# A fused attention and two-MoE kernel: six PSUM banks in one pool, other copies in the first MoE, a scaling moved in the last sum

## The chip, the cores and the metric

The kernel runs on one core of a Trainium2 chip. The metric is device time in microseconds of one execution; the value quoted is the median of three runs.

## The reference

Three stages follow each other. In the first, 4 batches of 12 heads with 448 rows of 64 are attended with two mixings across heads ("talking heads"); the second and third are dense two-layer blocks ("MoE" by name) over 1792 tokens of 768.

```python
scores = scale * np.matmul(q, k.transpose(0, 1, 3, 2))
scores = np.einsum('bhij,hg->bgij', scores, w_pre)
scores = scores - np.max(scores, axis=-1, keepdims=True)
attn = np.exp(scores)
attn = attn / (np.sum(attn, axis=-1, keepdims=True) + 1e-09)
attn = np.einsum('bhij,hg->bgij', attn, w_post)
attn_out = np.matmul(attn, v)
x = attn_out.transpose(0, 2, 1, 3).reshape(B * S, H * D)
h = x @ w_in                                     # 768 x 2048
g = np.where(h > 0.0, h, np.exp(np.minimum(h, 0.0)) - 1.0)
x = g @ w_out                                    # 2048 x 768
h = x @ w_in2                                    # 768 x 1024
sm = softmax(h); solu = h * sm
ln = (solu - mean) / np.sqrt(var + 1e-06) * g_ln
out = ln @ w_out2                                # 1024 x 768
```

## The kernel before

**Attention.** The 448 rows of a batch are cut into chunks of up to 120 rows (`CH`, 17 chunks in all). A chunk goes through five kinds of work on TensorE (PE), and each leaves its result in PSUM, from where ScalarE (ACT) or VectorE (DVE) takes it away.

- A *score* block (`add_score`, L574) multiplies q and k of two heads into two banks; two evacuations (`evac`, L580, tile `sev`) copy them out, on ACT or VectorE, and DMAs on SP's queue (`move`, L531, `sp<-sev`) spread them over partitions into the chunk's tile `sp`. `sev` has 8 buffers.
- A *pre* block (`pre`, L646, tile `pm`) mixes the heads for a unit of two groups of ten rows, again into two banks. VectorE takes the maxima (`top`, L651, tile `st`), ACT the exponentials (`expo`, L656, tile `e`, 10 buffers). There are 90 units.
- VectorE and GpSimd prepare the scaled second mixing (`weigh`, L667, tile `wr`).
- A *post* block (`post`, L679, tiles `po`) applies it, into two fixed banks; two copies (`take`, L687) put it into `at`.
- An *AV* block (L728, tile `av`) multiplies by v, two blocks to a chunk; a copy (L735, tile `x`) and a DMA send it to DRAM as `xs`.

Of the eight PSUM banks `ps_sc` has three (scores and AV), `ps_pm` three (pre) and `po` two. Each pool is a ring: the next tile takes the bank that was taken longest ago. In the first chunk scores use both pools in turn.

The order on every engine is written by a planner (`schedule`). Each operation has a rank (the time at which it is wished for), its engines with a cost in us, the operations it depends on, and the buffers it takes (`new`) or uses. The planner keeps a clock for each engine, and takes the next operation among the first 200 by rank that can start earliest. `ready` gives the time at which dependencies and buffers are free: the end of what frees them and a tail by engine (`tail`, 2.0 us for SP) plus `more`, or `lag` where it is given. What the planner thinks only sets the order; on the chip each engine waits on semaphores, in that order. The loads of q (`add_q`) and k (`add_k`) are such operations on SP's queue, with rank 9 and 4 us ahead of the score; q's was given `more=.5`, k's `lag=3.0`.

**First MoE** (function body after `schedule()`). The hidden units go in 8 groups (`fg`) of 256, the tokens in 4 blocks (`tb`) of 448. For each group and block `hid` (L377, tile `h`) makes two tiles of hidden units, `elu` (L388 to L393) works them, and `outp` (L883, tile `o`, four banks in a ring) makes six output tiles. For the first group ACT copies each `o` into the running sum `x1` (L897); for later groups VectorE adds it (L900). Between them the weights of the next groups are decoded by VectorE, ACT and GpSimd (`decode`, L218 to L231; `split`, L254; `wi_spill`, L286), a step at a time (`tick`, `paced`), by a running estimate of VectorE's time (`work`).

**Second MoE.** `hid2` (L1022), a normalisation, then for each of 7 pairs of token tiles seven products (`product`, L1094, tile `w`) in the order P1, P6, P7, P5, P4, P2, P3. `behind` adds them up into the four quarters of the output tile `ob` (L1112, L1114), scales a finished quarter by a value per token on ACT (L1117) and stores it by a DMA on SP's queue (L531).

Of the kernel before, what the change touches and what calls it, by code (L numbers as in the profile page):

```python
# [21 lines left out]
ECH = DM // 128  # L22
# [47 lines left out]
LEAD = 3  # L70

@with_exitstack
def kernel(ctx: ExitStack, tc: tile.TileContext, qa, kt, vt, wpre, wpost,
# [294 lines left out]
    def hid(fg, tb, ft, kcs=range(ECH)):  # L368
        wh, wl = w1[fg][0], w1[fg][1]
        xh, xl = xT[tb]  # L370
        if kcs[0] == 0:
            ring, p = ("sc", ps_sc) if (tb, ft) not in ((1, 1), (3, 1)) else ("h", ps_h)
            h_t[fg, tb, ft] = p.tile([128, 512], F32, tag=ring, name="h")
        ps = h_t[fg, tb, ft]
        for kc in kcs:
            for n, (a, x) in enumerate(((wh, xh), (wh, xl), (wl, xh))):
                nc.tensor.matmul(ps[:, :S], a[:, kc * FG + ft * 128:kc * FG + (ft + 1) * 128], x[:, kc, :],  # L377
                                 start=kc == 0 and n == 0, stop=kc == ECH - 1 and n == 2)
# [20 lines left out]
    class Buf:  # L399
        def __init__(self, ring):  # L400
            self.ring, self.users, self.at = ring, [], None
# [6 lines left out]
    bufs = {"sc": 3, "pm": 3, "po": 2, "sev": SB, "e": EB, "wr": WB, "st": 4, "kst": 2, "q": 4,  # L408
# [12 lines left out]
    def schedule():  # L421
# [14 lines left out]
        def ready(o, e):  # L436
            t = 0.0
            for d in o.deps:
                if d.end is None:
                    return None  # L440
                t = max(t, seen(d, e))
            more = dict.fromkeys(bufs, 0)
            for b in o.new:
                ring = rings[b.ring]
                n = bufs[b.ring] - more[b.ring]
                more[b.ring] += 1
                if b.at is None and len(ring) >= n:
                    for u in ring[-n].users:
                        if u.end is None:
                            return None  # L450
                        t = max(t, seen(u, e))
            return t

        while todo:
# [20 lines left out]
            if o.port and e in held:  # L475
                held[e] = o.end
            for b in o.new:
                if b.at is None:
                    b.at = o
                    rings[b.ring].append(b)  # L480
# [56 lines left out]
    def add_q(c, hf):  # L537

        qb_[c, hf] = Buf("q")
        r = t_sc[c, 6 * hf]  # L540

        def load(e):
            q_t[c, hf] = q_p.tile([128, 3, 128], F32, tag="q", name="q")
            dma(q_t[c, hf], qa[c, :, 3 * hf:3 * hf + 3])

        q_op[c, hf] = op(r - 9 if c > 1 else 4.0 + .1 * hf if c else [0.0, 3.0][hf], load, [], [qb_[c, hf]], sp=.5, more=.5)

    def add_k(b, h):
# [8 lines left out]
        k_op[b, h] = op(r0 - 4 if b else .5 + h * .6, load, [], [kb[b, h]], lag=3.0, **{"sp" if b or h % 4 == 0 else "act": .5})  # L557

    def add_score(c, h):
# [3 lines left out]
        ring = ("sc", "pm")[h // 2 % 2] if c == 0 else "sc"  # L563
        scb, svb = [Buf(ring) for _ in range(2)], [Buf("sev") for _ in range(2)]
# [3 lines left out]
        def mm(e):  # L568
            T[key] = [pools["ps_" + ring].tile([128, 512], F32, tag=ring, name="sc") for _ in range(2)]
# [63 lines left out]
    for u, sl in enumerate(units):  # L633
        eb, wb, sb = [Buf("e") for _ in range(2)], Buf("wr"), Buf("st")
        pmb, pob = [Buf("pm") for _ in range(2)], [Buf("po") for _ in range(2)]
# [5 lines left out]
        def pre(e, u=u, sl=sl):  # L641
            ps_t[u] = [ps_pm.tile([128, 512], F32, tag="pm", name="pm") for _ in range(2)]
# [63 lines left out]
    for c in range(NC):  # L706
# [12 lines left out]
        for n in range(2):  # L719
            r = t_av[c, n]  # L720
            xb, avb = Buf("x"), Buf("sc")

            def mm(e, c=c, n=n, w=w):
                ps = x_t[c, n] = ps_sc.tile([128, 512], F32, tag="sc", name="av")[:, :3 * w].rearrange("p (k w) -> p k w", k=3)
# [121 lines left out]
    for i in range(3):  # L846
        need_x = add_x(1, i, t_hid - 6 + 2 * i)
        add_w(3 + i, t_hid - 3 + 3 * i)
    for ft in range(2):
        o = None  # L850
        for p in range(3):
            o = op(t_hid + HD + ft * .01, lambda e, ft=ft, p=p: hid(0, 0, ft, range(2 * p, 2 * p + 2)),
                   need + [o] + [sc_ev[lc, h] for h in range(NH)], pe=HID / 3)
# [3 lines left out]
    schedule()  # L857
    spend(500)
# [12 lines left out]
    ps_o = pool("ps_o", 4, space=PSUM)  # L871
    def outp(fg, tb, rest):
# [3 lines left out]
        for e in range(ECH):  # L876
            run(1.21)
            ps = ps_o.tile([128, 512], F32, tag="o", name="o")
# [17 lines left out]
            if fg == 0:  # L896
                nc.scalar.copy(x1[tb][:, e, :], ps[:, :S])  # L897
            else:
# [197 lines left out]
    def behind(q, x):  # L1096
# [124 lines left out]
```

## Time and profile before

| | |
|---|---|
| median of three runs | 1047.11 us (1046.87 to 1049.83) |
| the profiled execution | 1046.41 us |
| its span, first to last instruction | 1044.6 us |
| granted TensorE clock, mean | 0.998 |
| PE busy / weight loads busy | 1021.1 / 859.6 us |
| VectorE / ACT / GpSimd busy | 732.6 / 556.1 / 286.2 us |
| chain that ended last, PE's share | 88% |

Busy time is what the instructions' records cover; overlapping records count once. On PE a record of a matmul begins where it starts and ends where a model ends it, so the distance between starts tells more than the length. "PEld" are the weight loads, which run beside the matmuls. A line with a wait names the waiting engine, the tile it was about to write and the line, and behind the arrow what was seen to release it; "issue" stands where nothing was seen. Attention fills the span up to about 360 us, the first MoE goes to about 821, the second from there on.

### The profile page before, as it was taken

To read this page: it belongs to the slowest core of one execution; us is meant where nothing else is said; L and a number is where in the kernel's file an instruction comes from. 1 tells how busy PE (TensorE), PEld (TensorE's weight loads), DVE (VectorE), ACT (ScalarE), POOL (GpSimd) and SP (SyncE) were. 2 spreads that over 40 slices of the span, in tenths; PEclk is the share of its full clock that TensorE was granted. 3 is DMA by queue.
4 is the path that set the end of the run, shared out by engine and by line. 5 is a ranking of instruction groups with operands and counts; after the bars stand their busy time and mean duration, and the time that the engine had idled before them with its cause. 6 is when DMAs were issued, how large, how long until landed. Compare 5 with 4: busy or idle time off the path is not lost.

```text
span 1044.6 us, 28451 instructions
## 1 busy us (share of the span) xinstructions
PE 1021.1 (98%) x11604; PEld 859.6 (82%) x11604; DVE 732.6 (70%) x1371; ACT 556.1 (53%) x1178; POOL 286.2 (27%) x297
## 2 busy tenths in 40 slices
PE   6899999999999999999999999999999999999998
PEld 2467777777666898999999999999999888889998
DVE  5687787677677357689978687786855355668874
ACT  3476677777677575544444345444444245555543
POOL 5011011111013524556534445444544200000000
PEclk9999999999999999999999999999999999999999
DMA  6776876776856542653523232423282533838741
GB/s 199 219 229 187 242 214 211 222 227 188 237 157 185 156 143 92 206 177 132 182 77 115 96 106 83 149 87 126 81 297 106 200 107 106 187 106 202 151 102 61
DMA packets 142442, 165.79 MB, mean 159 GB/s; under 512 B 79496, under 2 KB 119272, under 8 KB 142312
## 3 DMA queue, kind: packets, MB, share of 16 engines
q1 hardware_dynamic: 136207, 143.27, 46.2%
q0 software_dynamic: 3968, 17.30, 4.3%
q10 hardware_dynamic: 2137, 3.41, 1.1%
q8 instruction: 91, 1.49, 0.6%
q14 instruction: 39, 0.32, 0.1%
HBM read 88.02 MB, written 37.22 MB: 120 GB/s over the span
## 4 chain that ended last, share of the span: by engine, by line
PE 88%; DMA 3%; DVE 3%; ACT 3%; issue 2%; POOL 1%; SPq 0%; ACTq 0%; DVEq 0%; POOLq 0%
PE h L377 21%; PE o L883 21%; PE h L1022 11%; PE w L1094 10%; PE av L728 7%; PE po L679 7%; PE pm L646 6%; PE sc L574 6%; DMA sp<-sev 2%; ACT e L656 1%; DMA q<-in_qa_dram 1%; DVE st L651 1%; DVE wy L231 1%; ACT at L687 0%; DVE wq L227 0%
## 5 line engine op out<-in xcount | busy, mean ns | idle before, releaser
L656 ACT ACTIVATE e<-pm,st 128x448 f32<-128x448 f32 x180 | 113.7, 636 | 63.0 <-DVE st L651 54.7
L651 DVE TENSOR_REDUCE st<-pm 128x1 f32<-128x448 f32 x180 | 105.7, 617 | 54.6 <-PE pm L646 52.8
L883 PE MATMUL o<-gh,woh 128*128 128x448 f32 x384 | 140.6, 366 | 1.0 <-ACT x L897 0.8
L883 PE MATMUL o<-glo,woh 128*128 128x448 f32 x384 | 140.1, 365 | 0.0
L883 PE MATMUL o<-gh,wol 128*128 128x448 f32 x384 | 139.6, 363 | 0.0
L679 PEld LDWEIGHTS po<-wr,e 60*64 60x64 f32 x5040 | 101.0, 134 | 37.5 <-issue 23.8
L574 PE MATMUL sc<-kt,q 64*64 64x448 f32 x816 | 119.0, 559 | 9.2 <-DMA kt<-in_kt_dram 4.2
L900 DVE TENSOR_TENSOR x<-x,o 128x448 f32<-128x448 f32 x168 | 101.7, 613 | 28.7 <-PE o L883 27.7
L389 POOL TENSOR_TENSOR glo<-g,gh 128x448 fp32r<-128x448 f32 x64 | 83.3, 1301 | 124.6 <-ACT gh L388 122.2
L667 POOL TENSOR_TENSOR wr<-wpost_t,st 128x120 f32<-128x120 f32 x90 | 35.8, 398 | 281.8 <-DVE st L663 226.5
L646 PE MATMUL pm<-sp,wpre_t 64*64 64x448 f32 x720 | 108.6, 555 | 3.8 <-ACT e L656 2.3
L679 PE MATMUL po<-wr,e 60*64 60x60 f32 x5040 | 107.4, 219 | 3.4 <-issue 2.8
L377 PE MATMUL h<-xh,wih 128*128 128x448 f32 x288 | 105.4, 366 | 0.0
L377 PE MATMUL h<-xh,wil 128*128 128x448 f32 x288 | 105.1, 365 | 0.0
L377 PE MATMUL h<-xl,wih 128*128 128x448 f32 x288 | 104.7, 363 | 0.0
L1022 PE MATMUL h<-wi,x2h 128*128 128x512 f32 x308 | 98.7, 395 | 0.8 <-issue 0.8
L728 PEld LDWEIGHTS av<-at,v 128*64 128x64 f32 x1632 | 75.4, 137 | 15.0 <-issue 4.6
L393 DVE SCALAR_TENSOR_TENSOR g<-g,h 128x448 f32<-128x448 f32 x64 | 39.5, 616 | 66.0 <-ACT g L392 65.5
L728 PE MATMUL av<-at,v 128*64 128x120 f32 (+5 forms) x1632 | 82.6, 258 | 0.7 <-ACT x L735 0.5
L883 PEld LDWEIGHTS o<-gh,woh 128*128 128x128 f32 x384 | 72.1, 188 | 7.3 <-ACT x L897 1.4
L883 PEld LDWEIGHTS o<-glo,woh 128*128 128x128 f32 x384 | 72.0, 188 | 6.0
L883 PEld LDWEIGHTS o<-gh,wol 128*128 128x128 f32 x384 | 72.1, 188 | 5.6
(124 smaller groups left out, 1988.0 us busy)
## 6 DMA issues: line engine op xcount, KB each, us to landing
sp<-sev SPq DMA_DIRECT2D x93, 210.0 KB
ws<-in_wi_dram SPq DMA_DIRECT2D x33, 512.0 KB
ws<-in_wo_dram SPq DMA_DIRECT2D x21, 512.0 KB
lts<-sq SPq DMA_DIRECT2D x14, 512.0 KB
lt<-lts SPq DMA_DIRECT2D x56, 128.0 KB
q<-in_qa_dram SPq DMA_DIRECT2D x34, 192.0 KB
v<-in_vt_dram SPq DMA_DIRECT2D x24, 256.0 KB
wis<-ws POOLq DMA_DIRECT2D x12, 512.0 KB, 3.2
```

The lines of the kernel that those rows point to most:

```text
L377: nc.tensor.matmul(ps[:, :S], a[:, kc * FG + ft * 128:kc * FG + (ft + 1) * 128], x[:, kc, :], start=kc == 0 and n == 0, stop=kc == ECH - 1 ...
L389: nc.gpsimd.tensor_tensor(glo, g, f(gh), ALU.subtract)
L574: nc.tensor.matmul(T[key][i][64 * x:64 * x + 64, :S], q[sl, h % 6 // 2, 64 * x:64 * x + 64], k[sl, :], start=True, stop=True)
L646: nc.tensor.matmul(ps_t[u][r][64 * s:64 * s + 64, :S], wpre_t[p, :], sp_t[c][p, g, :], start=True, stop=True)
L651: nc.vector.tensor_reduce(out=st_t[u][:P, r:r + 1], in_=ps_t[u][r][:P, :S], op=ALU.max, axis=AX.X, negate=True)
L656: nc.scalar.activation(out=t[:P], in_=ps_t[u][r][:P, :S], func=AF.Exp, bias=st[:P, r:r + 1], scale=1.0, accum_out=st[:P, 2 + r:3 + r])
L679: nc.tensor.matmul(out[:, :, 5 * r:5 * r + 5], e_t[u, r][sl, 64 * n:64 * n + 64], wr_t[u][sl, r].rearrange("p (g a) -> p g a", a=5), start ...
L728: nc.tensor.matmul(ps[64 * k:64 * k + 64, i, :], v_t[CH[c][0]][:, 6 * n + 2 * i + k, q, :], at_t[c][:, q, 6 * n + 2 * i + k, :w], start=q ...
L883: nc.tensor.matmul(ps[:, :S], a[:, ft * DM + e * 128:ft * DM + (e + 1) * 128], x, start=n == 0, stop=n == 5)
L900: nc.vector.tensor_tensor(x1[tb][:, e, :], x1[tb][:, e, :], ps[:, :S], ALU.add)
L1022: nc.tensor.matmul(ps[:, hf * 512:hf * 512 + 512], a[:, k, :], w, start=n == 0, stop=n == 3 * ECH - 1)
L1094: nc.tensor.matmul(ps[:, :384], a[:, s, k, :], w, start=k == 0 and i == 0, stop=k == 3 and i == 2)
```

## The change

1. *Banks in attention.* The six banks of `ps_sc` and `ps_pm` become six named tiles of one buffer each (`bank0` to `bank5`), and the planner picks for each score, pre or AV block the banks that are free first, preferring banks last used by the same kind. Scores from the fourth chunk on, AV blocks after the first chunk's and pre blocks from the third chunk's first unit on may take any of the six; earlier ones stay in their half. Scores and AV together hold at most four banks, pre blocks at most four (`CAP`).
2. *Loads.* For chunks after the second, the planner counts 6.0 us (`QL`) from the end of a q load's issue to its use; the same for k loads after the first batch's.
3. *First MoE.* The hidden tiles take banks 0 to 2 in a named turn; the two first ones are operations with buffers. The four `o` banks are named in turn. The copies of `o` for the first group's token blocks 2 and 3 go to VectorE, with 0.55 in the running estimate.
4. *Last sum.* Behind P5, ACT scales the quarter c12 too; P3's product is then scaled and added in one VectorE instruction, and its ACT scaling is gone.

```diff
+CAP = 4
+QL = 6.0
...
-            ring, p = ("sc", ps_sc) if (tb, ft) not in ((1, 1), (3, 1)) else ("h", ps_h)
-            h_t[fg, tb, ft] = p.tile([128, 512], F32, tag=ring, name="h")
+            if home is not None:
+                h_t[fg, tb, ft] = home.tile()
+            elif (tb, ft) not in ((1, 1), (3, 1)):
+                h_t[fg, tb, ft] = ps_sc.tile([128, 512], F32, tag=f"bank{h_next[0]}", name="h", bufs=1)
+                h_next.append(h_next.pop(0))
+            else:
+                h_t[fg, tb, ft] = ps_h.tile([128, 512], F32, tag="h", name="h")
...
+        def tile(self):
+            p = pools["ps_sc" if self.bank < 3 else "ps_pm"]
+            return p.tile([128, 512], F32, tag=f"bank{self.bank}", name=self.ring, bufs=1)
+
+    banks = [None] * 6
+    most = {"sc": CAP, "pm": CAP}
...
-    bufs = {"sc": 3, "pm": 3, "po": 2, "sev": SB, "e": EB, "wr": WB, "st": 4, "kst": 2, "q": 4,
+    bufs = {"po": 2, "sev": SB, "e": EB, "wr": WB, "st": 4, "kst": 2, "q": 4,
...
+            asked = [b for b in o.new if b.ring in most]
+            if asked:
+                free_at = {}
+                for i, own in enumerate(banks):
+                    if own is None:
+                        free_at[i] = 0.0
+                    elif all(u.end is not None for u in own.users):
+                        free_at[i] = max(seen(u, e) for u in own.users)
+                kind = asked[0].ring
+                best = sorted((i for i in free_at if i in asked[0].only),
+                              key=lambda i: (max(free_at[i], t), banks[i] is not None and banks[i].ring != kind, free_at[i]))[:len(asked)]
+                if len(best) < len(asked):
+                    return None
+                t = max([t] + [free_at[i] for i in best])
+                rest = [i for i, own in enumerate(banks) if own is not None and own.ring == kind and i not in best]
+                over = len(asked) + len(rest) - most[kind]
+                if over > 0:
+                    ends = sorted(free_at[i] for i in rest if i in free_at)
+                    if len(ends) < over:
+                        return None
+                    t = max(t, ends[over - 1])
+                o.pick = best
...
-        q_op[c, hf] = op(r - 9 if c > 1 else 4.0 + .1 * hf if c else [0.0, 3.0][hf], load, [], [qb_[c, hf]], sp=.5, more=.5)
+        q_op[c, hf] = op(r - 9 if c > 1 else 4.0 + .1 * hf if c else [0.0, 3.0][hf], load, [], [qb_[c, hf]], sp=.5, lag=QL if c > 1 else 2.5)
...
-        pmb, pob = [Buf("pm") for _ in range(2)], [Buf("po") for _ in range(2)]
+        pmb, pob = [Buf("pm", range(0 if u >= first[2] else 3, 6)) for _ in range(2)], [Buf("po") for _ in range(2)]
...
-            xb, avb = Buf("x"), Buf("sc")
+            xb, avb = Buf("x"), Buf("sc", range(6 if c else 3))
...
-            if fg == 0:
+            if fg == 0 and tb < 2:
                 nc.scalar.copy(x1[tb][:, e, :], ps[:, :S])
+            elif fg == 0:
+                work(.55, pe_t + .1)
+                nc.vector.tensor_copy(x1[tb][:, e, :], ps[:, :S])
...
-        nc.vector.tensor_tensor(dst, ps, src, ALU.add)
+        if x == "P3":
+            nc.vector.scalar_tensor_tensor(dst, ps, col(9, t), src, ALU.mult, ALU.add)
+        else:
+            nc.vector.tensor_tensor(dst, ps, src, ALU.add)
         if x == "P5":
             nc.vector.tensor_tensor(c12, ps, c12, ALU.add)
+            nc.scalar.activation(out=c12, in_=c12, func=AF.Copy, scale=col(9, t))
...
-            nc.scalar.activation(out=dst, in_=dst, func=AF.Copy, scale=col(9, tt))
+            if x != "P3":
+                nc.scalar.activation(out=dst, in_=dst, func=AF.Copy, scale=col(9, tt))
```

The planner's new order shows on PE, here in attention around the first AV block of the twelfth chunk (88 rows). `sc<-kt,q` are score blocks (x4 is one block), `pm` pre blocks, `po` the first rows of a post block, `av` AV blocks. Before:

```order
L646 MATMUL pm<-sp,wpre_t 64x448 x4
L679 MATMUL po_108<-wr,e 64x12x5
...
L574 MATMUL sc<-kt,q 64x448 x4
L646 MATMUL pm<-sp,wpre_t 64x448 x4
L728 MATMUL av<-at,v 64x88 x24
L646 MATMUL pm<-sp,wpre_t 64x448 x4
L679 MATMUL po_108<-wr,e 64x12x5
...
L574 MATMUL sc<-kt,q 64x448 x4
```

With the change, a little ahead of the same place (an AV block's tile is named `sc` there as well, and x8 are two blocks):

```order
L616 MATMUL sc<-kt,q 64x448 x8
L721 MATMUL po_108<-wr,e 64x12x5
...
L688 MATMUL pm<-sp,wpre_t 64x448 x4
L616 MATMUL sc<-kt,q 64x448 x8
L721 MATMUL po_108<-wr,e 64x12x5
...
L688 MATMUL pm<-sp,wpre_t 64x448 x4
L770 MATMUL sc<-at,v 64x120 x24
```

Before, a pre block follows nearly every post block and scores come singly; now scores come in pairs, and pre blocks move against post blocks.

On VectorE in the first MoE, from the first group's third token block on (`x` and `x_2` are the running sums, `ws`, `wq`, `wy` a weight being decoded, `g` the hidden units). Before:

```order
L231 SCALAR_TENSOR_TENSOR wy<-wy,wq 128x512
L218 TENSOR_SCALAR ws<-ws 128x512
L393 SCALAR_TENSOR_TENSOR g<-g,h 128x448
L223 TENSOR_SCALAR wq<-ws 128x512
L227 SCALAR_TENSOR_TENSOR wq<-ws,wq 128x512
```

With the change:

```order
L229 SCALAR_TENSOR_TENSOR wq<-ws,wq 128x512
L946 COPY x_2_6992<-o 128x448
L233 SCALAR_TENSOR_TENSOR wy<-wy,wq 128x512
L946 COPY x_2_6992<-o 128x448
L402 SCALAR_TENSOR_TENSOR g<-g,h 128x448
L946 COPY x_2_6992<-o 128x448
L220 TENSOR_SCALAR ws<-ws 128x512
```

The copies now stand between the decode steps, one to a step.

On ACT at the end of the program, the last pair's products (`ob<-ob,sm` is the scaling, `ob<-w` the first product's copy). Before:

```order
L1080 CAST lA_11253<-lt 128x512
L1117 ACTIVATE ob<-ob,sm 128x384
L1080 CAST lS_11254<-sl 128x512
L1105 COPY ob<-w 128x384
L1117 ACTIVATE ob<-ob,sm 128x384 x4
```

With the change:

```order
L1129 CAST lA_11253<-lt 128x512
L1129 CAST lS_11254<-sl 128x512
L1154 COPY ob<-w 128x384
L1167 ACTIVATE ob<-ob,sm 128x384
L1171 ACTIVATE ob<-ob,sm 128x384 x3
```

Of the last four scalings the first is now that of c12 behind P5, and none follows P3.

## Rows read from the trace of the kernel before

**Rows 1.** The page, busy us (share of the span) xinstructions.
```profile
PE 1021.1 (98%) x11604; PEld 859.6 (82%) x11604; DVE 732.6 (70%) x1371; ACT 556.1 (53%) x1178; POOL 286.2 (27%) x297
```
**Rows 2.** Stretches: us; busy (x) of PE, PEld, DVE, ACT, POOL; clock, DMA share, GB/s.
```profile
500.00:600.00 100.00, 100.00 (x495) 92.57 (x494) 79.47 (x122) 42.69 (x80) 48.08 (x42) 1.00 0.35 115
```
**Rows 3.** Timeline of PE in attention: start us, us, engine, line, what.
```profile
142.37 0.99 PE L679 MATMUL po<-wr,e 60*64 60x60 f32 x56
143.18 0.94 PE L574 MATMUL sc<-kt,q 64*64 64x448 f32 x8
143.94 1.20 PE L646 MATMUL pm<-sp,wpre_t 64*64 64x448 f32 x8
144.69 1.26 PE L574 MATMUL sc<-kt,q 64*64 64x448 f32 x8
```
**Rows 4.** The chain that ended last, one AV block: start us, us, what.
```profile
155.41 2.61 PE av L728 x48
```
**Rows 5.** Stretch 65 to 345 us: PE and PEld of L574, L646, L679, L728; all instructions.
```profile
65.00:345.00 280.00, 85.95 (x616) 28.88 (x616) 1.00 0.71 209
65.00:345.00 280.00, 92.50 (x632) 27.95 (x632) 1.00 0.71 209
65.00:345.00 280.00, 94.86 (x4429) 89.35 (x4429) 1.00 0.71 209
65.00:345.00 280.00, 71.12 (x1344) 64.90 (x1344) 1.00 0.71 209
65.00:345.00 280.00, 275.52 (x7022) 197.09 (x7023) 208.02 (x528) 201.12 (x533) 40.08 (x84) 1.00 0.71 209
```
**Rows 6.** Waits of the weight loads, 65 to 345 us: us in total, times, longest.
```profile
PEld po L679 <- issue: 21.0, 77, 1.1
PEld pm L646 <- issue: 9.7, 46, 0.2
PEld pm L646 <- ACT e L656: 6.5, 19, 0.9
...
PEld sc L574 <- ACT sev L580: 2.3, 7, 0.5
...
PEld sc L574 <- DVE sev L580: 0.7, 2, 0.5
```
**Rows 7.** Timeline of PE, a pre block at 329 us; in brackets the idle time before.
```profile
329.11 0.54 PE L646 MATMUL pm<-sp,wpre_t 64*64 64x448 f32 x1
329.82 0.98 PE L646 MATMUL pm<-sp,wpre_t 64*64 64x448 f32 x6 [0.18 <-ACT e L656]
```
**Rows 8.** The chain that ended last, loads of q.
```profile
185.81 4.24 DMA q<-in_qa_dram
...
282.34 3.67 DMA q<-in_qa_dram
```
**Rows 9.** Waits of PE, 345 to 470 us.
```profile
PE o L883 <- ACT x L897: 0.8, 1, 0.8
```
**Rows 10.** Groups by line: busy us, mean ns of one, idle us before.
```profile
L897 ACT COPY x<-o 128x448 f32<-128x448 f32 x24 | 12.5, 536 | 1.7 <-PE o L883 1.5
L580 DVE COPY sev<-sc 128x448 f32<-128x448 f32 x87 | 52.6, 615 | 11.4 <-PE sc L574 11.1
```
**Rows 11.** Stretch 395 to 425 us, columns as in rows 2.
```profile
395.00:425.00 30.00, 29.15 (x144) 26.63 (x143) 20.34 (x33) 19.07 (x38) 18.04 (x14) 1.00 0.35 123
```
**Rows 12.** Timeline of the end of the program.
```profile
1040.51 0.56 DVE L1112 TENSOR_TENSOR ob<-w,ob 128x384 f32<-128x384 f32 x1 [1.52 <-PE w L1094]
1041.10 0.61 ACT L1117 ACTIVATE ob<-ob,sm 128x384 f32<-128x384 f32 x1 [1.46 <-DVE ob L1112]
1041.74 0.33 SPq L531 DMA_DIRECT2D out_dram<-ob  x1
```
**Rows 13.** Waits of ACT, 0 to 65 us.
```profile
ACT sev L580 <- DMA sp<-sev: 5.2, 3, 2.2
```

More of the change, by code (lines that the diff above doesn't have):

```diff
@@ L366, with hid @@
     h_t, g_t = {}, {}
-    def hid(fg, tb, ft, kcs=range(ECH)):
+    h_next = []
+    def hid(fg, tb, ft, kcs=range(ECH), home=None):
         wh, wl = w1[fg][0], w1[fg][1]
@@ L399, with __init__ @@
     class Buf:
-        def __init__(self, ring):
-            self.ring, self.users, self.at = ring, [], None
+        def __init__(self, ring, only=range(6)):
+            self.ring, self.users, self.at, self.only = ring, [], None, only
+        def tile(self):
[3 more added lines that the diff above has]
+    most = {"sc": CAP, "pm": CAP}
     class Op:
@@ L442, in ready @@
             more = dict.fromkeys(bufs, 0)
+            asked = [b for b in o.new if b.ring in most]
[20 more added lines that the diff above has]
+                o.pick = best
             for b in o.new:
+                if b.ring in most:
+                    continue
                 ring = rings[b.ring]
@@ L476, in schedule @@
                 held[e] = o.end
+            for b, i in zip((b for b in o.new if b.ring in most), getattr(o, "pick", ())):
+                b.bank, banks[i] = i, b
             for b in o.new:
@@ L479, in schedule @@
                     b.at = o
-                    rings[b.ring].append(b)
+                    if b.ring not in most:
+                        rings[b.ring].append(b)
             o.emit(e)
@@ L556, in add_k @@
         r0 = t_sc[HEAD[b] - 1, h] if b else 0.0
-        k_op[b, h] = op(r0 - 4 if b else .5 + h * .6, load, [], [kb[b, h]], lag=3.0, **{"sp" if b or h % 4 == 0 else "act": .5})
+        k_op[b, h] = op(r0 - 4 if b else .5 + h * .6, load, [], [kb[b, h]], lag=QL if b else 3.0, **{"sp" if b or h % 4 == 0 else "act": .5})
     def add_score(c, h):
@@ L562, in add_score @@
         n = 5 * G
-        ring = ("sc", "pm")[h // 2 % 2] if c == 0 else "sc"
-        scb, svb = [Buf(ring) for _ in range(2)], [Buf("sev") for _ in range(2)]
+        scb, svb = [Buf("sc", range(3 * (h // 2 % 2 if c == 0 else 0), 6 if c > 2 else 3 * (1 + (h // 2 % 2 if c == 0 else 0)))) for _ in range(2)], [Buf("sev") for _ in range(2)]
         r = t_sc[c, h]
@@ L568, in mm @@
         def mm(e):
-            T[key] = [pools["ps_" + ring].tile([128, 512], F32, tag=ring, name="sc") for _ in range(2)]
+            T[key] = [b.tile() for b in scb]
             q, k = q_t[c, h // 6], kt_t[b, h]
@@ L639, with pre @@
                 at_ops[c] = []
-        def pre(e, u=u, sl=sl):
-            ps_t[u] = [ps_pm.tile([128, 512], F32, tag="pm", name="pm") for _ in range(2)]
+        def pre(e, u=u, sl=sl, pmb=pmb):
+            ps_t[u] = [b.tile() for b in pmb]
             for s, (c, g) in enumerate(sl):
@@ L720, with mm @@
             r = t_av[c, n]
-            xb, avb = Buf("x"), Buf("sc")
-            def mm(e, c=c, n=n, w=w):
-                ps = x_t[c, n] = ps_sc.tile([128, 512], F32, tag="sc", name="av")[:, :3 * w].rearrange("p (k w) -> p k w", k=3)
+            xb, avb = Buf("x"), Buf("sc", range(6 if c else 3))
+            def mm(e, c=c, n=n, w=w, avb=avb):
+                ps = x_t[c, n] = avb.tile()[:, :3 * w].rearrange("p (k w) -> p k w", k=3)
                 for i in range(3):
@@ L848 @@
         add_w(3 + i, t_hid - 3 + 3 * i)
+    hb = [Buf("sc", range(3)) for _ in range(2)]
     for ft in range(2):
@@ L851 @@
         for p in range(3):
-            o = op(t_hid + HD + ft * .01, lambda e, ft=ft, p=p: hid(0, 0, ft, range(2 * p, 2 * p + 2)),
-                   need + [o] + [sc_ev[lc, h] for h in range(NH)], pe=HID / 3)
+            o = op(t_hid + HD + ft * .01, lambda e, ft=ft, p=p: hid(0, 0, ft, range(2 * p, 2 * p + 2), hb[ft]),
+                   need + [o] + [sc_ev[lc, h] for h in range(NH)], [] if p else [hb[ft]], [hb[ft]] if p else [], pe=HID / 3)
+    for b in hb:
+        b.users.append(Op())
     for i in range(3):
@@ L857 @@
     schedule()
+    h_next += [3 - sum(b.bank for b in hb)] + [b.bank for b in hb]
     spend(500)
@@ L870 @@
     ps_h = pool("ps_h", 1, space=PSUM)
-    ps_o = pool("ps_o", 4, space=PSUM)
+    ps_o = pool("ps_o", 1, space=PSUM)
     def outp(fg, tb, rest):
@@ L877, in outp @@
             run(1.21)
-            ps = ps_o.tile([128, 512], F32, tag="o", name="o")
+            ps = ps_o.tile([128, 512], F32, tag=f"o{(tb * ECH + e) % 4}", name="o")
             n = 0
```

## The prediction

> **What bounds the kernel now.** The first view is the busy table of the page [rows 1]: PE is busy for 1021.1 of 1044.6 us, with its weight loads at 859.6. Taken at its word that leaves 23.5 us to gain in the whole program. The table by stretches says where not to look: from 500 to 600 us PE is busy for 100.00 of 100 us [rows 2], and the chain of waits is PE's own matmuls, block after block of 7.28 us, up to the end. Those stages can gain only at their borders.
>
> Attention is another matter, because a matmul's record there also covers time in which the next one could not start. So I read the distance from one block's start to the next one's on PE's timeline [rows 3]: a post block (L679, 56 records) takes 143.18 - 142.37 = 0.81 us, a score block (L574, 8 records) 0.76, a pre block (L646, 8 records) 0.75, and an AV block (L728, 48 records) of 120 columns 2.61 in the chain [rows 4]. Between 65 and 345 us stand 616, 632, 4429 and 1344 records of these four lines [rows 5], which is 77, 79, 79 and 28 blocks; the 28 AV blocks are those of 14 chunks with 1574 columns in all, so 112 columns and 2.61 x 112/120 = 2.44 us each. At those distances they need 58.5 + 59.3 + 64.1 + 68.3 = 250 us. The stretch lasts 280. **PE loses about 30 us there**, although its busy sum is 275.52.
>
> [...]
>
> What the 30 us wait for is in the waits of the weight loads [rows 6]. A pre block waits for ACT's exponential 6.5 us in 19 waits: its bank is still being read. A score block waits for its evacuations, 2.3 us (ACT) and 0.7 us (VectorE). The larger sums are named "issue" (po 21.0 us in 77, pm 9.7 us in 46), where no releaser is seen. One bank wait can be watched at 329.11 us [rows 7]: one matmul of a pre block starts, the next only at 329.82, after ACT's exponential.
>
> **The change part by part.**
>
> *Banks, attention.* Before, a pre block takes two of three banks, so one of them was last used by the pre block just before it. I counted, from the order of PE's instructions with the distances above, how much PE work stands between the last writer of a bank that a pre block needs and that pre block. Under 2.0 us (two short blocks) it was in 49 of 89 cases; with the changed turn it is in 13 of 90, of which 10 follow a score. That leaves 13/49 of the 6.5 us: **-4.8 us**. For score blocks the cases with under 1.0 us fall from 34 of 87 to 17 of 100, half of the 3.0 us: **-1.5 us**. The post banks do not change (two), and neither does the number of evacuations; cases under 1.6 us between posts go from 40 to 33 of 89, which I count as nothing, covered by the same two engines (they are busy 208 and 201 of the 280 us [rows 5]). The bounds of this edit: nothing, if the next wait stands right behind; and if the 9.7 us of pm "issue" are bank waits too and fall likewise, another 9.7 x 36/49 = 7.1.
>
> *Lag of q and k loads.* The planner counted 0.5 + 2.5 = 3.0 us from the issue of a q load to its use (3.5 for k); now 6.5 for both. The loads keep their ranks; the scores that need them move back. In the chain two q loads took 4.24 and 3.67 us from issue to landing [rows 8], so they were 1.2 and 0.7 us later than planned, and a late load stops all of PE behind its score. I take **-2.0 us**. Bounds: nothing, and both landings whole, 7.9. If a score is now put too late, what is late next is the chunk's pre block; in the new order 8.5 us or more of PE work stand between a chunk's last score and its first pre block from the third chunk on (7.2 before), so there is cover.
>
> *Copies of token blocks 2 and 3.* 12 copies leave ACT (0.54 us each) for VectorE, where a copy of the same shape from PSUM takes 0.615 [rows 10]: 6.4 us less on ACT, 7.4 more on VectorE, between 395 and 425 us. There ACT is busy 19.07 and VectorE 20.34 of 30 us [rows 11]; VectorE goes to 27.7, with decode work of later weights behind it that has until the next group of hidden units. What PE loses there is one wait for such a copy on ACT, 0.8 us [rows 9], since the copy stood behind a decode step that waited for GpSimd. I take **-0.8**. If VectorE comes late instead, the nearest price is the same wait with the sign turned: +0.8.
>
> [...]
>
> *Named banks in the first MoE.* The turn of the banks of h and o is the ring's turn of before; nothing, since PE is dense there [rows 2].
>
> *Last sum.* For each pair of token tiles one ACT scaling moves from behind P3 to behind P5, and P3's addition becomes one instruction with a multiplication. At the end of the program VectorE's last addition starts at 1040.51, ACT's scaling at 1041.10 and the store's issue at 1041.74 [rows 12]; now the store follows VectorE: 1041.74 - 1041.10 = **-0.6 us**. The moved scaling lies beside matmuls; the fused form I price as the plain addition (0.56 us).
>
> *Startup, before 65 us.* Other orders, the same waits for the first loads and moves: nothing, bounds 2 us either way.
>
> **Sum:** -4.8 - 1.5 - 2.0 - 0.8 - 0.6 = -9.7. The profiled execution took 1046.4 us, so 1036.7. The median of the three runs is 0.7 above it: **1037.4**.
>
> **The rivals.**
>
> *The waits only change their name.* Evacuations and exponentials run on two engines in fixed order, each over 70% busy [rows 5], so more banks might only let PE run ahead and stop at the post block. For it speaks that "issue" before post blocks is the largest sum [rows 6]; against it, that the new order has pre blocks further ahead of their post blocks (a quarter of the cases have under 8.9 us of PE work between, before 5.4). Then only the loads' term by half, the copies and the end remain: 1.0 + 0.8 + 0.6 = 2.4 us, 1044.7.
>
> *More than forecast.* The unnamed pm waits were bank waits: 7.1 us more, 1030.3.
>
> *Slower: the ring of eight score buffers.* Scores now come in bursts: 20 double and one triple row of scores on PE where there were two doubles. The copy out of a score's banks needs one of eight buffers, free only when the move four score blocks earlier has landed. Cases with under 6 us of PE work over these four blocks go from 8 to 21 of 92, under 4 us from 3 to 10. Such a wait stops ACT or VectorE, with exponentials behind it. Its price stands in the startup, where ACT waited 5.2 us in 3 waits for a move [rows 13], 1.7 each. If the 13 new cases cost 1.2 us each, that is 15.6 us, and 1037.4 + 15.6 = 1053. It decides from 9.7/13 = 0.75 us each. Against it: the eight close cases of before show no such wait after 65 us.
>
> *The change does not do what it says:* the printed orders show that it does, double pre blocks among it; only its bank rule could be idle in the first three chunks, where it is meant to be.
>
> **How the numbers follow.** I give the forecast 0.50, "more" 0.13, "waits change their name" 0.25 and the slower case 0.12. A measurement here tells about 0.3%, 3.1 us, from no change. The forecast and "more" are faster by over that; of the 0.25 I put 0.09 there and 0.16 within it. That gives 0.72, 0.16 and 0.12. The range runs from 1030, where "more" lies, to 1047, which takes in the renamed waits at their worst (nothing gained); the slower case and a little on the fast side stay out.
>
> **What would show it.** Right: between 65 us and the last AV block PE's records take about 8 us less; pm's wait for ACT's exponential falls under 2.5 us; no q load in the chain; the wait of o for the copy is gone; the last store is issued right behind VectorE, with the last ACT scaling a tile earlier. Wrong: waits of ACT or VectorE copies for the moves sp<-sev after 65 us (the ring), post blocks waiting longer for at copies (renamed waits), or a wait of o for VectorE between 395 and 425 us.

## The result, and the profile after

The changed kernel took 1057.44 us (median of 8 runs, 1051.36 to 1061.98); the kernel before took 1049.17 beside it on the same chip (8 runs, 1046.87 to 1051.66). The ratio is 1.0085 (in brackets here and below the 95% interval: [1.0060, 1.0109]): **slower by 0.85%**, where 1037.4 and faster was forecast. The profiled execution of the changed kernel took 1055.98 us, its span is 1054.2, 9.6 more than before.

The page of the changed kernel, busy time of the engines and shares of the chain that ended last:

```profile
PE 1021.3 (97%) x11604; PEld 869.2 (82%) x11604; DVE 737.2 (70%) x1377; ACT 557.2 (53%) x1174; POOL 278.4 (26%) x295
PE 82%; DVE 6%; DMA 4%; issue 3%; ACT 2%; POOL 2%; ACTq 0%; SPq 0%; DVEq 0%; POOLq 0%
```

PE is busy as long as before (1021.3 against 1021.1 us, [rows 1]). VectorE gained 4.6 us of work. The chain says more: PE's share of it fell from 88% to 82%, VectorE's rose from 3% to 6% and DMA's from 3% to 4%.

To find the place, I take for each stretch its length less what its blocks need at the distances of [rows 3, 4]; in the first MoE its length less the matmuls of `h` and `o` times 7.285/36 us (a block of 7.28 us has 36). AV blocks of fewer columns, and the 512-column matmuls at the start of the second MoE, are priced by their columns, which is an estimate: in the chain of the kernel before, AV blocks of 110, 98, 88 and 80 columns take 2.41, 2.17, 1.97 and 1.81 us where their columns give 2.39, 2.13, 1.91 and 1.74, and those of 40 columns 1.53 where they give 0.87 (two of these lie between 20 and 65 us in both kernels, so both losses there can come out up to 1.3 us high, but not their difference); the 512-column matmuls start 0.23 us apart there (849.68 and 850.37 on PE's timeline, for three), as 7.285/36 x 512/448 gives. An example, 150 to 345 us of the changed kernel: 432 records of L616, 448 of L688, 3136 of L721 and 951 of L770 are 54, 56, 56 and 19.8 blocks (AV blocks at 2.44 us), which need 41.0 + 42.0 + 45.4 + 48.3 = 176.7 us; 195 - 176.7 = 18.3 are lost. What PE loses by stretch, in us:

| | 20-65 | 65-150 | 150-345 | 345-420 | 420-545 | 545-835 |
|---|---|---|---|---|---|---|
| before | 14.0 | 8.0 | 21.9 | 3.1 | 0.3 | 1.2 |
| after | 18.0 | 9.0 | 18.3 | 1.0 | 6.6 | 5.7 |

The differences are +4.0, +1.0, -3.6, -2.1, +6.3 and +4.5, together +10.1, and the end gives back 0.5 (below): 9.6, the whole difference of the spans (the first 20 us hold the same 90 matmul records in both). So **the loss stands in two places**, the first MoE (+10.8) and the startup (+4.0), and attention from 150 us on did get faster.

The first MoE, the changed kernel by stretches, columns as in [rows 2]; the second row lies where the stretch of [rows 2] does, the third at the border to the second MoE:

```profile
425.00:455.00 30.00, 28.31 (x137) 25.26 (x137) 26.20 (x40) 13.08 (x24) 15.67 (x13) 1.00 0.47 158
485.00:545.00 60.00, 57.91 (x285) 52.78 (x284) 53.83 (x80) 27.29 (x49) 30.40 (x24) 1.00 0.45 154
800.00:830.00 30.00, 26.57 (x123) 24.12 (x123) 18.13 (x30) 10.63 (x19) 17.31 (x18) 0.94 0.28 105
```

PE is no longer dense there. Who ends its waits, in the list of PE's waits over the whole span (waiting tile and line, releaser: us, times, longest):

```profile
PE o L929 <- DVE x L949: 7.7, 6, 3.4
PE sc L616 <- ACT sev L622: 4.2, 5, 1.6
...
PE pm L688 <- ACT e L698: 1.9, 1, 1.9
```

The output tile `o` waits 7.7 us for VectorE's additions, a wait that the kernel before did not have. What VectorE does around the first of these waits is on its timeline:

```profile
428.97 0.65 DVE L220 TENSOR_SCALAR ws<-ws 128x512 f32<-128x512 f32 x1 [0.79 <-DMA ws<-in_wi_dram]
...
432.02 0.61 DVE L949 TENSOR_TENSOR x<-x,o 128x448 f32<-128x448 f32 x1
...
433.68 0.61 DVE L402 SCALAR_TENSOR_TENSOR g<-g,h 128x448 f32<-128x448 f32 x1
434.22 0.60 DVE L949 TENSOR_TENSOR x<-x,o 128x448 f32<-128x448 f32 x1
437.18 0.50 DVE L220 TENSOR_SCALAR ws<-ws 128x512 f32<-128x512 f32 x1 [2.35 <-DMA ws<-in_wi_dram]
437.60 1.14 DVE L949 TENSOR_TENSOR x<-x,o 128x448 f32<-128x448 f32 x2
```

PE's first wait, 1.42 us, ends at 432.68 with the addition of 432.02. That addition stood behind a decode step (L220, the first on a weight tile `ws`) which had waited 0.79 us for its tile's load, and behind the two steps that follow it. At 435 us VectorE is not overworked either, it stands still: the next such step is at the head of its queue and waits 2.35 us for a load; the additions that free the banks of `o` stand behind it, and two come at once when it is through (PE's wait behind this one was 0.20 us, at 449.30). The chain that ended last runs through the same load, and through another near the end of the stage (start, us, what):

```profile
429.65 2.96 DMA wis<-ws
...
432.74 4.33 DMA ws<-in_wi_dram
...
437.18 0.50 DVE ws L220
437.68 1.06 DVE x L949 x2
...
807.38 3.17 DMA ws<-in_wo_dram
...
810.65 1.20 DVE ws L220
...
816.00 1.01 POOL ws L336
...
817.04 0.57 DVE wg L322
...
819.85 0.54 DVE x L949
```

The load at 432.74 could not start before the spill `wis<-ws` had freed its tile (it landed at 429.65 + 2.96 = 432.61). Near the end it is not the load alone: the chain goes on through GpSimd, for which VectorE's next decode step (L322) waited 2.33 us, and only then comes the addition that PE waits for. Between 425 and 545 us VectorE waits 4 times for loads of this kind, 4.7 us, in the changed kernel:

```profile
DVE ws L220 <- DMA ws<-in_wi_dram: 4.7, 4, 2.4
```

In the kernel before it was once (and once more, 0.7 us, for a load from `in_wo_dram`):

```profile
DVE ws L218 <- DMA ws<-in_wi_dram: 1.6, 1, 1.6
```

### The profile page after: what moved, and what is told of

The parts are those of the page before. It is cut to its first block, busy times and chain, and to the rows that moved or that the text cites. A ratio compares the mean times of both kernels' runs of the same rounds, so it can differ in the third digit from the quotient of the medians.

```text
span 1054.2 us, 28461 instructions
## 1 busy us (share of the span) xinstructions
PE 1021.3 (97%) x11604; PEld 869.2 (82%) x11604; DVE 737.2 (70%) x1377; ACT 557.2 (53%) x1174; POOL 278.4 (26%) x295
## 4 chain that ended last, share of the span: by engine, by line
PE 82%; DVE 6%; DMA 4%; issue 3%; ACT 2%; POOL 2%; ACTq 0%; SPq 0%; DVEq 0%; POOLq 0%
PE o L929 16%; PE h L386 16%; PE h L1071 11%; PE w L1143 10%; PE sc L770 8%; PE po L721 7%; PE sc L616 7%; PE pm L688 6%; DMA sp<-sev 1%; DVE wq L229 1%; DVE ws L220 1%; DVE wy L233 1%; DVE wq L225 1%; DMA ws<-in_wi_dram 1%; PE sc L386 1%
## 5 line engine op out<-in xcount | busy, mean ns | idle before, releaser
L721 PEld LDWEIGHTS po<-wr,e 60*64 60x64 f32 x5040 | 99.8, 135 | 35.8 <-issue 21.3
L616 PE MATMUL sc<-kt,q 64*64 64x448 f32 x816 | 109.3, 569 | 11.0 <-ACT sev L622 4.2
L693 DVE TENSOR_REDUCE st<-pm 128x1 f32<-128x448 f32 x180 | 106.0, 616 | 19.8 <-PE pm L688 18.3
L721 PE MATMUL po<-wr,e 60*64 60x60 f32 x5040 | 103.3, 220 | 6.8 <-issue 3.9
L386 PE MATMUL h<-xh,wih 128*128 128x448 f32 x276 | 100.8, 365 | 0.0
L386 PE MATMUL h<-xh,wil 128*128 128x448 f32 x276 | 100.7, 365 | 0.0
L386 PE MATMUL h<-xl,wih 128*128 128x448 f32 x276 | 100.3, 363 | 0.0
L688 PE MATMUL pm<-sp,wpre_t 64*64 64x448 f32 x720 | 96.8, 548 | 2.3 <-ACT e L698 1.9
L770 PEld LDWEIGHTS sc<-at,v 128*64 128x64 f32 x1632 | 76.9, 139 | 15.4 <-ACT e L698 4.2
L770 PE MATMUL sc<-at,v 128*64 128x120 f32 (+5 forms) x1632 | 84.0, 260 | 1.2 <-issue 1.2
L729 DVE COPY at<-po 128x480 f32<-128x480 f32 x84 | 54.3, 652 | 30.0 <-PE po L721 29.3
```

The source lines that it names most:

```text
L616: nc.tensor.matmul(T[key][i][64 * x:64 * x + 64, :S], q[sl, h % 6 // 2, 64 * x:64 * x + 64], k[sl, :], start=True, stop=True)
L693: nc.vector.tensor_reduce(out=st_t[u][:P, r:r + 1], in_=ps_t[u][r][:P, :S], op=ALU.max, axis=AX.X, negate=True)
L721: nc.tensor.matmul(out[:, :, 5 * r:5 * r + 5], e_t[u, r][sl, 64 * n:64 * n + 64], wr_t[u][sl, r].rearrange("p (g a) -> p g a", a=5), start ...
L770: nc.tensor.matmul(ps[64 * k:64 * k + 64, i, :], v_t[CH[c][0]][:, 6 * n + 2 * i + k, q, :], at_t[c][:, q, 6 * n + 2 * i + k, :w], start=q ...
```

## The experiments

Eleven kernels ran, each against the kernel before on the same chip. The first four take apart what the change does in the first MoE: the copies on another engine, their 0.55 us in the running estimate by which decode steps are placed, the named banks, and whatever attention hands on.

**The copies go back to ACT** (all else as changed):

```diff
-            if fg == 0 and tb < 2:
+            if fg == 0:
                 nc.scalar.copy(x1[tb][:, e, :], ps[:, :S])
-            elif fg == 0:
-                work(.55, pe_t + .1)
-                nc.vector.tensor_copy(x1[tb][:, e, :], ps[:, :S])
```

> The changed kernel with the copies of token blocks 2 and 3 back on ACT (and without their 0.55 in the running estimate); all else as changed. The profile of the change puts the loss into waits of o for VectorE's additions: 6.6 us between 425 and 545 us and 5.2 around 820. Theories that blame the copies (their load on VectorE, or their count in the estimate) expect both gone: about 1046.5 against 1046.4 for the kernel before, since attention there came out 0.5 us worse and the end 0.6 better. A theory that blames the named banks of h and o expects the waits to stay: 1056.

Measured: 1046.27 us (10 runs; before 1047.56), ratio 0.9988 [0.9965, 1.0012]. The stretches 420 to 545 and 545 to 835 lose 0.1 us each. All of the first MoE's loss comes with the copies; the named banks, still in this kernel, cost nothing.

**The copies alone** (the kernel before, with the branch above added):

> The kernel before with nothing but the copies of token blocks 2 and 3 on VectorE, with their 0.55 in the estimate. Theories that blame the copies: 10 to 11 us slower than before, with the waits of o for VectorE at the same places. Named banks: no difference, 1046.

Measured: 1059.90 us (4 runs), ratio 1.0099 [1.0067, 1.0132]; 6.6 and 4.1 us lost in the two stretches. Its list of PE's waits repeats the changed kernel's row to the digit:

```profile
PE o L883 <- DVE x L903: 7.7, 6, 3.4
```

**The copies on VectorE, but not counted** (the changed kernel without one line):

```diff
-                work(.55, pe_t + .1)
```

> The changed kernel with the copies on VectorE, but their 0.55 us not counted in the running estimate, so the decode steps keep their places in VectorE's order. If the load itself (12 copies of 0.61 us) makes the waits, it stays at about 1056. If the count pushed decode steps behind additions, the waits go and it comes to 1045 to 1047.

Measured: 1049.47 us (10 runs), ratio 1.0004 [0.9980, 1.0028]. VectorE does the same 12 copies, and 425 to 545 us is nearly whole again: the wait of `o` is down to

```profile
PE o L929 <- DVE x L945: 1.8, 2, 1.1
PE o L929 <- DVE x L948: 0.6, 1, 0.6
```

L948 are the additions, L945 the copies themselves: `o` waits for these twice, 1.8 us, between 417 and 420 us.

**Counted, but not moved** (the kernel before; the copies stay on ACT):

```diff
+            elif fg == 0:
+                work(.55, pe_t + .1)
+                nc.scalar.copy(x1[tb][:, e, :], ps[:, :S])
```

> The kernel before with the copies on ACT, where they were, but with 0.55 us counted for each on VectorE: decode steps move as in the change, VectorE has no copy more. Load theory: no difference from before, 1046 to 1048. Count theory: 9 to 11 us slower, with waits of o for VectorE between 425 and 545 us and near 820.

Measured: 1056.98 us (10 runs), ratio 1.0077 [1.0055, 1.0100], 9.4 us over the kernel before beside it. No instruction changed its engine, and the wait is there:

```profile
PE o L883 <- DVE x L903: 7.5, 6, 3.4
```

These four settle it. The order of VectorE's instructions says how: of the decode steps of VectorE, 43, 91, 132, 171, 208, 247, 284 stood ahead of the first addition of the second to eighth group in the kernel before and in the uncounted one; in the changed kernel, the counted one and the one with the copies alone it is 39, 87, 129, 164, 203, 240, 276. **Four steps, one weight piece, fall behind in the first group; they are not made up, and at the last group eight are missing.** Each piece is then finished later, its tile is free later, the next load into it starts later, and the step that needs this load waits at the queue's head. At the end of the stage the rest is drained at once: 12 steps instead of 5 stand between the first additions of the last group's second and third block, and there PE waits longest, on the changed kernel's timeline:

```profile
820.44 0.47 PE L929 MATMUL o<-gh,woh 128*128 128x448 f32 x1 [3.43 <-DVE x L949]
```

**Only the banks: the old lags of q and k** (copies on ACT, `QL` taken out):

```diff
-        q_op[c, hf] = op(r - 9 if c > 1 else 4.0 + .1 * hf if c else [0.0, 3.0][hf], load, [], [qb_[c, hf]], sp=.5, lag=QL if c > 1 else 2.5)
+        q_op[c, hf] = op(r - 9 if c > 1 else 4.0 + .1 * hf if c else [0.0, 3.0][hf], load, [], [qb_[c, hf]], sp=.5, lag=2.5)
...
-        k_op[b, h] = op(r0 - 4 if b else .5 + h * .6, load, [], [kb[b, h]], lag=QL if b else 3.0, **{"sp" if b or h % 4 == 0 else "act": .5})
+        k_op[b, h] = op(r0 - 4 if b else .5 + h * .6, load, [], [kb[b, h]], lag=3.0, **{"sp" if b or h % 4 == 0 else "act": .5})
```

> The changed kernel with the copies back on ACT and with the old lags of q and k loads: banks and last sum alone. In the profiles so far the changed attention loses about 4 us less of PE than before between 150 and 345 us (18.2 to 19.3 us in three profiles against 21.9 to 23.4 in three) and about 4 more between 20 and 65 (16.2 to 19.2 against 13.4 to 14.2). If banks make both, this shows both, and comes to 1046 to 1048. If the lags make the steady gain, the loss between 150 and 345 us is back at 22 and the time at 1050 or so.

Measured: 1057.53 us (6 runs), ratio 1.0087 [1.0058, 1.0116]. Both theories missed it. From 150 to 345 us it loses only 16.7 us, the least of all; from 20 to 65 and from 65 to 150 it loses 19 each. Its waits of PE name the loads:

```profile
PE sc L616 <- DMA q<-in_qa_dram: 6.6, 2, 5.0
```

**Only the lags** (the kernel before with `QL`):

> The kernel before with the lag of 6.0 us for q and k loads alone. If the lags are worth the 2.0 us of the forecast: 1045, and no q load in the chain that ended last. If the banks make all: no difference, 22 us lost between 150 and 345 us. If the lags made the loss of the startup: 4 us more between 20 and 65 us.

Measured: 1046.65 us (10 runs), ratio 0.9990 [0.9969, 1.0011]: nothing that can be told. With the old banks the lags bring nothing; with the early open banks they are worth 1057.5 - 1046.3 = 11.2 us.

**The banks opened later** (copies on ACT):

```diff
-        scb, svb = [Buf("sc", range(3 * (h // 2 % 2 if c == 0 else 0), 6 if c > 2 else 3 * (1 + (h // 2 % 2 if c == 0 else 0)))) for _ in range(2)], [Buf("sev") for _ in range(2)]
+        scb, svb = [Buf("sc", range(3 * (h // 2 % 2 if c == 0 else 0), 6 if c > 4 else 3 * (1 + (h // 2 % 2 if c == 0 else 0)))) for _ in range(2)], [Buf("sev") for _ in range(2)]
...
-        pmb, pob = [Buf("pm", range(0 if u >= first[2] else 3, 6)) for _ in range(2)], [Buf("po") for _ in range(2)]
+        pmb, pob = [Buf("pm", range(0 if u >= first[4] else 3, 6)) for _ in range(2)], [Buf("po") for _ in range(2)]
...
-            xb, avb = Buf("x"), Buf("sc", range(6 if c else 3))
+            xb, avb = Buf("x"), Buf("sc", range(6 if c > 2 else 3))
```

> The changed kernel with the copies back on ACT, and the six banks open to all only from the fifth chunk's units, the sixth chunk's scores and the fourth chunk's AV blocks on; the first chunks stay in their halves as before. If the startup is lost because early blocks compete for all banks, the loss between 20 and 65 us returns to about 14 and the steady gain stays: about 4 us less than before, 1043. If the changed startup is only another order with the same waits (chance), the time stays at that of the copies back, 1046.

Measured: 1043.28 us (12 runs), ratio 0.9947 [0.9925, 0.9969], **faster**. It loses 12.3 us from 20 to 65 (before 14.0), and 19.6 from 150 to 345.

The startup can be watched in the clock. The changed kernel from 40 to 60 us and two short pieces, columns as in [rows 2] (the clock is the third number from the end):

```profile
40.00:60.00 20.00, 18.18 (x372) 10.52 (x368) 11.43 (x29) 10.76 (x28) 1.16 (x3) 0.83 0.68 216
...
38.00:40.00 2.00, 2.00 (x29) 1.33 (x25) 1.15 (x2) 0.03 (x1) 0.00 (x0) 0.50 0.74 216
...
46.00:48.00 2.00, 2.00 (x30) 1.52 (x32) 0.28 (x1) 1.23 (x4) 0.00 (x0) 0.50 0.65 233
```

The wait ahead of it, on its PE's timeline:

```profile
35.98 1.62 PE L688 MATMUL pm<-sp,wpre_t 64*64 64x448 f32 x5 [1.86 <-ACT e L698]
```

The kernel with the banks opened later, the same stretch and the same block of its PE's timeline:

```profile
40.00:60.00 20.00, 19.00 (x492) 13.60 (x492) 15.39 (x39) 12.91 (x36) 2.34 (x6) 1.00 0.73 221
```
```profile
35.95 1.22 PE L688 MATMUL pm<-sp,wpre_t 64*64 64x448 f32 x5 [0.87 <-ACT e L698]
```

In the changed kernel a pre block stands 1.86 us, and behind it PE's granted clock is at 0.50 of full speed from about 37 to 40 and again from 44 to 50 us. All five kernels with the early opening show a granted clock of 0.50 somewhere between 32 and 52 us; the kernel before and the seven others show 1.00 in all slices of 10 and 15 us from 30 to 65. The slices of the changed kernel between 36 and 50 us add up to 5.0 us of full clock not granted (2 us times what is missing to 1.00). That is a bound, since PE would have waited for part of it anyway, and it is of the size of the +4.0 there. The other kernels say the same. From 30 to 54 us the clock that was not granted, in slices of 2 us, and what the startup (20 to 65 us) loses more than in the kernel before:

| early opening, kernel | clock not granted, us | lost more, us |
|---|---|---|
| changed | 5.1 | 4.0 |
| copies back on ACT | 1.7 | 2.2 |
| copies not counted | 5.1 | 5.2 |
| old lags | 5.1 | 5.0 |
| ten score buffers (below) | 3.4 | 3.6 |

The other eight miss nothing there. The kernel with the old lags misses another 5.1 us between 66 and 78 (its mean clock, 0.990 over a span of 1055.9 us, leaves 10.6 in all), around its two longest waits there (3.0 us for a copy and 5.0 for q), so part of its 11.2 us goes the same way.

**Old lags with the late banks**, to see whether the lags matter there:

> The kernel with the banks opened later (copies on ACT, new last sum), but with the old lags of q and k loads. If the lags only mend what early opening breaks, this equals the kernel with banks opened later, 1043. If open banks need the lags everywhere, because scores then run ahead of their loads, it loses more than 3 us between 65 and 345 us, with PE waiting for q, as with early banks and old lags.

Measured: 1045.68 us (10 runs), ratio 0.9983 [0.9956, 1.0010]. The intervals overlap with those of the longer lags, so this is not decided; the profile loses 11.2 us from 65 to 150 against 7.1. One late load is seen there, of k and not of q: PE waits 2.16 us for it at 71.6 us.

**At most three banks a kind** (late banks, `CAP = 3`):

> The kernel with the banks opened later, but with at most three banks to each kind instead of four: any bank may be taken, yet a pre block still has to wait for one bank of the pre block just before it. If the steady gain (150 to 345 us: 19.6 us lost with four, 21.9 before) comes from the fourth bank, it goes: pm waits for ACT's exponential return to 6 us, and the time to 1046 to 1048. If the free choice of a bank makes it: 1043.

Measured: 1047.77 us (10 runs), ratio 1.0019 [1.0000, 1.0038]: the gain of the late banks is gone, as the theory of the fourth bank says. But the sign it named missed. The pre blocks' wait for the exponential is not back at 6 us:

```profile
PEld pm L688 <- ACT e L698: 0.8, 3, 0.4
```

So the gain needs the fourth bank, but it is not the wait whose name falls.

**Ten score buffers** (`SB = 10`), first with the early banks, then with the late ones:

> The changed kernel with the copies back on ACT, and ten buffers for copied scores instead of eight. If the startup's extra loss (16 to 19 us of PE between 20 and 65 us against 14) comes from copies that wait for a buffer of that ring (4.0 us in ACT and 2.8 in VectorE before 65 us with the copies back), it falls to about 14 and the time to 1043. If it comes from the order of early blocks alone, it stays: 1046.

> The kernel with the banks opened later, and ten buffers for copied scores. Ring theory: little left to gain, since only 2.5 us of such waits are left: 1041 to 1043. No theory expects it slower than 1044.

Measured: 1050.36 us (10 runs), ratio 1.0024 [1.0001, 1.0046], and 1039.55 us (10 runs, 1035.81 to 1043.90), ratio 0.9927 [0.9906, 0.9948]. Both are outside what was expected of them, the first above, the second below. With early banks the buffers do not repair the startup: it still loses 17.6 us, with one wait of PE of 2.59 us for an exponential and the clock at 0.50 from about 41 to 47 us. From 65 to 345 us it loses 33 us, more than the kernel before, so the gain in the steady part seems to hang on the order that the planner happens to find. With late banks this is **the fastest kernel of the study**, 0.73% under the kernel before; its interval overlaps that of eight buffers, so what the two more buffers add is not decided.

## Why the prediction was wrong, by its steps

**Copies of token blocks 2 and 3: this is the step that failed.** It priced -0.8 us and held that the decode work behind the copies "has until the next group". The load itself was as foreseen:

```profile
395.00:425.00 30.00, 30.00 (x150) 27.72 (x149) 26.29 (x40) 13.13 (x24) 13.17 (x10) 1.00 0.26 89
```

VectorE is busy 26.29 us (27.7 forecast), ACT 13.13, and PE is busy all 30.00. The prediction's wrong sign, a wait of `o` in just this stretch, would have stayed silent: the loss comes behind 425 us. What was not priced is the 0.55 in the estimate, quoted in the change. I read it as bookkeeping; it is an order to put the decode steps later. The slack "until the next group" was the slack of one group; the arrears are kept for all eight. With the copies it cost 11.2 us (1057.4 against 1046.3); the first MoE's loss by its PE is 10.8 against before. The longer copies from PSUM (0.61 us each on VectorE in the changed kernel, 0.53 on ACT) are not told from nothing: with the count gone, the copies on VectorE give 1049.47 against 1046.27, whose ratios' intervals overlap. The wrong sign does come in that kernel, 1.8 us of waits for the copies where one for ACT's took 0.8 before; a loss of 1.0 us, near the +0.8 priced for a late VectorE, is not excluded.

**Banks, attention (-4.8 and -1.5 forecast).** The waits fell nearly as foreseen. The weight loads' waits, 65 to 345 us of the changed kernel, answer [rows 6]:

```profile
PEld po L721 <- issue: 18.9, 62, 1.7
PEld pm L688 <- issue: 6.4, 28, 0.6
...
PEld sc L770 <- ACT e L698: 4.2, 6, 0.7
...
PEld po L721 <- POOL wr L709: 3.1, 3, 1.6
PEld pm L688 <- ACT e L698: 3.0, 9, 0.6
PEld sc L616 <- ACT e L698: 3.0, 3, 2.5
...
PEld sc L616 <- ACT sev L622: 1.2, 6, 0.2
```

Rows of the kernel before that stand against these, beside [rows 6]:

```profile
PEld po L679 <- ACT at L687: 5.4, 21, 0.4
...
PEld po L679 <- POOL wr L667: 1.8, 7, 0.4
...
PEld av L728 <- ACT e L656: 1.4, 2, 0.7
```

A pre block waits 3.0 us for the exponential, 9 times (6.5 in 19 before; 1.7 would have been the counted share, and the sign asked for under 2.5), a score 1.2 us for its evacuations (3.0 before). So 5.3 of the 6.3 us left these rows. Three rows took 7.1 back: scores now wait 3.0 us for an exponential, the AV blocks (L770), which may now take a pre block's bank, 4.2 instead of 1.4, and the post blocks' wait for `wr` is up from 1.8 to 3.1. What fell beside them are rows that the prediction had left alone: the post blocks' wait for copies (5.4 to 1.9) and the two "issue" rows (30.7 to 25.3 together). What stays is measured best between kernels of one kind: from 65 to 345 us the four kernels with the old order of banks lose 29.6 to 34.0 us, mean 31.1; the changed kernel and the two with its attention lose 26.0 to 29.4, mean 27.6. **The gain is 3.5 us, not 8.3** (with the loads). These profiles of one order scatter by 4 us, and the early banks with ten buffers, another order, lose 33 us there, so the size is rough.

The rival of the renamed waits is right by a part, then. Its sign, longer waits of post blocks for copies, did not come (ACT `at` 1.9 us, before 5.4); the copies' own waits for post blocks grew instead (ACT's from 2.3 to 13.1 us, and VectorE's), which says that VectorE and ACT run ahead and stand:

```profile
DVE at L729 <- PE po L721: 26.3, 28, 2.9
```

In the kernel before this was:

```profile
DVE at L687 <- PE po L679: 8.0, 13, 1.1
```

**Startup (0, bounds 2 either way).** Out of bounds: 4.0 us lost here in the changed kernel, 2.2 and 5.2 in the two with the same attention. "The same waits" was wrong: between 28 and 50 us PE stands 1.86 and 1.61 us in single waits, before 1.27 at most, and its clock is at 0.50 behind them. That the planner's order there runs ahead of the first moves is my reading, which no run tests by itself. This takes away all that the rest of attention gains: without the copies' count the kernel is as fast as before.

**Lag of q and k loads (-2.0).** Alone nothing, 0.9990 [0.9969, 1.0011], though no q load is left in that kernel's chain; in the changed kernel one is, at 93.66 us, where the sign asked for none. That two loads came 1.2 and 0.7 us later than planned was no price of theirs in the end. The prediction costed this edit apart; it belongs to the banks, which without it lose 11.2 us.

**Named banks in the first MoE (0).** Right: 0.1 us lost in each stretch with them.

**Last sum (-0.6).** Right. The end of the changed kernel's timeline answers [rows 12]:

```profile
1050.65 0.62 DVE L1162 SCALAR_TENSOR_TENSOR ob<-w,sm,ob 128x384 f32<-128x384 f32 x1 [1.59 <-PE w L1143]
```

No scaling follows it; from its start to the end of the span are 1054.2 - 1050.65 = 3.55 us, before 1044.6 - 1040.51 = 4.09, so 0.5 less. The fused form takes 0.62 us where 0.56 was assumed.

**The rival of the ring of eight buffers** had the right sign and not the cause. After 65 us the copies wait 3.0 us for moves (it needed 9.7 to decide, and priced 15.6):

```profile
ACT sev L622 <- DMA sp<-sev: 0.3, 1, 0.3
DVE sev L622 <- DMA sp<-sev: 2.7, 1, 2.7
```

**What stays open.** Which wait ends last for PE in the startup with early banks (ten buffers did not remove it), and by what path three banks a kind lose the gain, were not settled. That the halved clock makes most of the startup's loss is argued from sizes that go together in five kernels; no run changed the clock alone.

## What to carry to other kernels

Where a program's order is fixed by a running estimate, an entry in that estimate is a change of its own, and is priced by what it moves behind it: print the order, and count for each consumer how many steps now stand ahead of it, up to the end of the stage and not only where the edit stands. A step that waited for a load at the head of an engine's queue held up everything behind it (2.35 us here), so a queue with idle time to spare can still hold up another engine (VectorE was busy for 26.20 of 30 us from 425 to 455, and PE waited 1.42 us for it). And more freedom for a planner (buffers, banks) is to be tried stage by stage: here it paid in the steady part in most orders, and lost as much in the startup until it was opened later.

## What the runs showed of the hardware

PE's granted clock fell after some of PE's waits, which I had not expected behind a stage that is dense otherwise, and held after others just as long. The changed kernel at the end of the first MoE:

```profile
816.00:820.00 4.00, 1.00 (x5) 0.58 (x4) 1.33 (x3) 1.65 (x4) 2.92 (x4) 1.00 0.26 103
...
822.00:824.00 2.00, 2.00 (x6) 1.75 (x6) 1.75 (x4) 1.81 (x3) 1.16 (x2) 0.50 0.00 0
...
826.00:828.00 2.00, 2.00 (x12) 1.85 (x11) 1.20 (x2) 0.00 (x0) 1.59 (x1) 1.00 0.00 0
```

PE was busy for 1.00 of 4 us up to 820; from 822 to 824 its clock is 0.50, and from 826 it is 1.00 again. Its matmuls start 0.37 us apart at the lower level (822.15, 822.52, 822.89 on its timeline) and 0.20 us apart at the higher (826.16, 826.37, 826.57), so of the 2 us of this slice I estimate that 2 x (1 - 0.20/0.37), about 0.9, are lost, on top of the wait of 3.43 us.

The kernel with the copies alone and the one that only counts them have the same wait in the same stretch, 3.4 us; in the second it ends at 817.60. There the clock stays at 1.00, over the 30 us from 805 to 835 of both and in these slices of 2 us, first of the copies alone, then of the counted kernel, where it begins 1.4 us behind the wait:

```profile
827.00:829.00 2.00, 2.00 (x12) 1.61 (x10) 2.00 (x5) 1.93 (x3) 1.29 (x2) 1.00 0.00 0
```
```profile
819.00:821.00 2.00, 2.00 (x11) 1.82 (x10) 2.00 (x5) 1.64 (x3) 1.00 (x1) 1.00 0.00 0
```

The startup shows the same. A wait of 1.86 us in the changed kernel was followed by the lower level, one of 1.91 us in the kernel that does not count its copies, at the same block (36.07 us), by 1.00 up to 40 us. So the length of a single wait did not decide it here, and what did is open.
